# K and V transposed by one crossbar DMA per head and batch, in place of TensorE and VectorE, in the forward and backward of two attention blocks

## The chip, the cores and the metric

The kernel runs on one core of one Trainium2 chip. The metric is the device time of one execution in microseconds (us). The kernel before takes 1850.8 us (median of four runs, 1850.6 to 1851.6). Executions of one kernel mostly agree within 0.3%. Ratios in this text are computed as the mean time of one kernel's fast runs over the mean of the other's fast runs of the same rounds, so they are not quite the ratio of the medians quoted beside them.

Names: PE is TensorE (matrix products), DVE is VectorE, ACT is ScalarE, POOL is GpSimd, SP is SyncE. SP computes nothing here: it issues DMAs, in order. "SPq" in a profile is SP's instruction queue. The packets of every queue are recorded on the same 16 DMA engines, with the number of their queue (q1 is SP's, q0 GpSimd's). "Rings" in this text is the author's word for the packets of a queue that wait there; no record shows how full they are. L243 is line 243 of the kernel whose profile is shown; the numbers shift a little from kernel to kernel.

## The reference, cut to what matters

Two independent attention blocks A and B of the same shape, forward and backward. Per block there are B = 8 batches, H = 32 heads, 96 queries, 512 keys, Dh = 128, D = 640, all bfloat16.

```python
def _A_ref(x, k_cache, v_cache, wq, wo):
    q = (x @ wq).reshape(B, Sq, H, Dh).transpose(0, 2, 1, 3)
    scores = jnp.einsum("bhqd,bhkd->bhqk", q, k_cache) * (Dh ** -0.5)
    p = softmax(scores)
    o = jnp.einsum("bhqk,bhkd->bhqd", p, v_cache)
    return o.transpose(0, 2, 1, 3).reshape(B, Sq, H * Dh) @ wo
# outputs: concat(A, B), and the gradients of x, k_cache, v_cache, wq, wo of each block
```

There are 2 x 32 x 8 = 512 pairs of a head and a batch. Each needs its K and V both as loaded (keys on the partitions) and transposed (Dh on the partitions), because the products that give the scores and dP contract over Dh.

## The kernel before

The kernel is a software pipeline. Every (head, batch) passes through stages s1 to s8, one "tick" apart, and a scheduler then fixes the order of the instructions on each engine. The parts that the change and the argument touch:

```python
def c_ld(h, b):                       # SP's queue: two loads of 128 KB
    K_sb = kvp.tile([128, KC, 128], BF16, name="K_sb", bufs=11)
    V_sb = kvp.tile([128, KC, 128], BF16, name="V_sb", bufs=8)
    nc.sync.dma_start(K_sb[:], kc[b, h].rearrange("(p c) d -> p c d", c=KC))
    nc.sync.dma_start(V_sb[:], vc[b, h].rearrange("(p c) d -> p c d", c=KC))
def c_s1(h, b):                       # eight PE transposes, one DVE copy
    kvT_ps = bank([128, 2 * Sk], BF16, "kvT_ps")
    for c in range(KC):
        nc.tensor.transpose(kvT_ps[:, c * 128:(c + 1) * 128], st["K_sb"][:, c, :], ident[:])
    for c in range(KC):
        nc.tensor.transpose(kvT_ps[:, Sk + c * 128:Sk + (c + 1) * 128], st["V_sb"][:, c, :], ident[:])
    KVT = wk.tile([128, 2 * Sk], BF16, name="KVT", bufs=5)
    nc.vector.tensor_copy(KVT[:], kvT_ps[:])
    # ... st["KT"], st["VT"] are the halves of KVT
def c_s2a(h, b):                      # the first use of KVT
    nc.tensor.matmul(S_ps[:], hs["QT_h"][:, tok], st["KT"], start=True, stop=True)
    # ...
def c_s6(h, b):                       # the last use of KVT
    nc.tensor.matmul(dP_ps[:], hs["dOT_h"][:, tok], st["VT"], start=True, stop=True)
    # ...
def c_s4(h, b):                       # c_s7 does the same for dK
    # ... dV_ps by PE
    nc.scalar.activation(dV_sb[:], dV_ps[:], ACT.Identity, scale=1.0)
    nc.sync.dma_start(dv[b, h].rearrange("(p c) d -> p (c d)", c=KC), dV_sb[:])   # SP's queue again
```

So SP issues four DMAs of 128 KB for each head and batch: loads of K and V, stores of dV and dK. GpSimd's queue carries the weights, dwq, dwo and the outputs.

Of the kernel before, what the change touches and what calls it, by code (L numbers as in the profile page):

```python
# [11 lines left out]
BF16 = mybir.dt.bfloat16  # L12
# [32 lines left out]
OFF = dict(ld=0, s1=2, s2=3, s3=3, s4=4, s5=5, s6=6, s7=7, s8=8)  # L45
# [5 lines left out]
SLOTS = dict(LOAD=0, S2A=5, S2B=5.5, S1=6, S8=10, S7=20, S5=30, S4=40, S6=50, S3A=52, S3B=53, S5B=54, HEAD=SL_HEAD, GRP=SL_GRP)  # L51


def build_block(tc, em, tick0, blk, x, kc, vc, wq, wo, g_all, out_all, dx, dk, dv, dwq, dwo, ident, ones, pools, HG=8, first=True, groups=None):
    nc = tc.nc
    B, Sq, D = x.shape
    _, H, Sk, Dh = kc.shape
# [5 lines left out]
    KC = Sk // 128  # L63
# [28 lines left out]
    const, ps, kvp, wk, hd, hst, grp = (pools[k] for k in ("const", "ps", "kvp", "wk", "hd", "hst", "grp"))  # L92

    def bank(shape, dt, name):
        return ps.tile(shape, dt, name=name, tag="bank")
# [4 lines left out]
    CS = pools["CS"]  # L100
# [62 lines left out]
    def pA(h):  # L163
        def f():
            wo_h = hd.tile([128, D], BF16, name="wo_h", bufs=1)
            nc.gpsimd.dma_start(wo_h[:], wo[h * 128:(h + 1) * 128, :])
            wq_h = hd.tile([128, DC, 128], BF16, name="wq_h", bufs=1)
            with nc.allow_non_contiguous_dma(reason="per-head wq slice"):
                nc.gpsimd.dma_start(wq_h[:], wq_v[:, :, h * 128:(h + 1) * 128])
            HS[(blk, h)] = dict(wo_h=wo_h, wq_h=wq_h)  # L170
        return f

    def pB(h):
        def f():
            st = HS[(blk, h)]
            woT_ps = bank([128, DC * 128], BF16, "woT_ps")
            for c in range(DC):
                nc.tensor.transpose(woT_ps[:, c * 128:(c + 1) * 128], st["wo_h"][:, c * 128:(c + 1) * 128], ident[:])
            woT_h = hd.tile([128, DC * 128], BF16, name="woT_h", bufs=1)
            evac(EV["pB0"], woT_h[:], woT_ps[:])  # L180
            st["woT_h"] = woT_h
            wqT_ps = bank([128, DC * 128], BF16, "wqT_ps")
            for c in range(DC):
                nc.tensor.transpose(wqT_ps[:, c * 128:(c + 1) * 128], st["wq_h"][:, c, :], ident[:])
            wqT_h = hst.tile([128, D], BF16, name="wqT_h")
            evac(EV["pB1"], wqT_h[:], wqT_ps[:])
            st["wqT_h"] = wqT_h
            st["OT_h"] = hst.tile([128, T], BF16, name="OT_h")
            st["dQT_h"] = hst.tile([128, T], BF16, name="dQT_h")
            st["QT_h"] = hd.tile([128, T], BF16, name="QT_h")  # L190
            st["dOT_h"] = hd.tile([128, T], BF16, name="dOT_h")
        return f

    def pC(h, which, si):
        def f():
            st = HS[(blk, h)]
            (t0, w) = tsplits[si]
            if which == 0:
                dst = st["QT_h"]
                lhs = lambda c: st["wq_h"][:, c, :]  # L200
                rhsT = S["xT"]
                sc = scale
            else:
                dst = st["dOT_h"]
                lhs = lambda c: st["woT_h"][:, c * 128:(c + 1) * 128]
                rhsT = S["gT"]
                sc = None
            q_ps = bank([128, w], F32, "q_ps")
            for c in range(DC):
                nc.tensor.matmul(q_ps[:], lhs(c), rhsT[:, c, t0:t0 + w], start=(c == 0), stop=(c == DC - 1))  # L210
            evac(EV["pC%d%d" % (which, si)], dst[:, t0:t0 + w], q_ps[:], sc)
        return f
# [15 lines left out]

    def c_ld(h, b):
        def f():  # L230
            K_sb = kvp.tile([128, KC, 128], BF16, name="K_sb", bufs=11)
            V_sb = kvp.tile([128, KC, 128], BF16, name="V_sb", bufs=8)
            nc.sync.dma_start(K_sb[:], kc[b, h].rearrange("(p c) d -> p c d", c=KC))
            nc.sync.dma_start(V_sb[:], vc[b, h].rearrange("(p c) d -> p c d", c=KC))
            CS[(blk, h, b)] = dict(K_sb=K_sb, V_sb=V_sb)
        return f

    def c_s1(h, b):
        def f():
            st = CS[(blk, h, b)]  # L240
            kvT_ps = bank([128, 2 * Sk], BF16, "kvT_ps")
            for c in range(KC):
                nc.tensor.transpose(kvT_ps[:, c * 128:(c + 1) * 128], st["K_sb"][:, c, :], ident[:])  # L243
            for c in range(KC):
                nc.tensor.transpose(kvT_ps[:, Sk + c * 128:Sk + (c + 1) * 128], st["V_sb"][:, c, :], ident[:])  # L245
            KVT = wk.tile([128, 2 * Sk], BF16, name="KVT", bufs=5)
            nc.vector.tensor_copy(KVT[:], kvT_ps[:])  # L247
            st["KT"] = KVT[:, 0:Sk]
            st["VT"] = KVT[:, Sk:2 * Sk]
        return f  # L250

    def c_s2a(h, b):
# [23 lines left out]
    def c_s3a(h, b):  # L276
        def f():
            with tc.high_priority(PRIO_OFF):
                st = CS[(blk, h, b)]
                rinv = wk.tile([Sq, 1], F32, name="rinv", bufs=3)  # L280
                nc.vector.reciprocal(rinv[:], st["rowsum"][:])  # L281
                st["rinv"] = rinv
        return f
# [214 lines left out]
    for g in range(NG):  # L498
        h0 = GH0[g]
        for hh in range(groups[g]):  # L500
            h = h0 + hh
            c0t = tick0 + h * B
            em.add(c0t + HK["pA"], SL_LOAD, pA(h))
            em.add(c0t + HK["pB"], SL_HEAD, pB(h))
            for si in range(NTS):
                em.add(c0t + HK["pC0"][min(si, len(HK["pC0"]) - 1)], SL_HEAD, pC(h, 0, si))
                em.add(c0t + HK["pC1"][min(si, len(HK["pC1"]) - 1)], SL_HEAD, pC(h, 1, si))
            em.add(c0t + HK["pD1"], SL_HEAD, pD(h, 1))
            em.add(c0t + HK["pD0"], SL_HEAD, pD(h, 0))
            for b in range(B):  # L510
                ct = c0t + b
                em.add(ct + OFF["ld"], SLOTS["LOAD"], c_ld(h, b))
                em.add(ct + OFF["s1"], SLOTS["S1"], c_s1(h, b))
                em.add(ct + OFF["s2"], SLOTS["S2A"], c_s2a(h, b))
                em.add(ct + OFF["s2"], SLOTS["S2B"], c_s2b(h, b))
                em.add(ct + OFF["s3"], SLOTS["S3A"], c_s3a(h, b))
                em.add(ct + OFF["s3"], SLOTS["S3B"], c_s3b(h, b))
                em.add(ct + OFF["s5"], SLOTS["S5B"], c_s5b(h, b))
                em.add(ct + OFF["s4"], SLOTS["S4"], c_s4(h, b))
                S45.setdefault(ct + OFF["s5"], [None, None, None])[0] = (blk, h, b)  # L520
                S45.setdefault(ct + OFF["s4"], [None, None, None])[1] = (blk, h, b)
                S45.setdefault(ct + OFF["s6"], [None, None, None])[2] = (blk, h, b)
                S78.setdefault(ct + OFF["s8"], [None, None])[0] = (blk, h, b)
                S78.setdefault(ct + OFF["s7"], [None, None])[1] = (blk, h, b)
                em.add(ct + OFF["s6"], SLOTS["S6"], c_s6(h, b))
                em.add(ct + OFF["s7"], SLOTS["S7"], c_s7(h, b))
            em.add(c0t + HK["qA0"], SL_HEAD, qA(h, 0))
            for di in range(len(dsplits)):
                em.add(c0t + HK["qB"][min(di, len(HK["qB"]) - 1)], SL_HEAD + 1, qB(h, di))
            em.add(c0t + HK["qA1"], SL_HEAD, qA(h, 1))  # L530
            qd_parts = HK["qD"]
            for (k_, c_lo, c_hi) in qd_parts:
                if c_lo < DC:
                    em.add(c0t + k_, SL_HEAD + 2, qD(h, c_lo, min(c_hi, DC)))
        cLg = tick0 + (h0 + groups[g] - 1) * B + B - 1
        gs0 = max(3, (GSPREAD0 * groups[g]) // HG)
        gs1 = max(3, (GSPREAD1 * groups[g]) // HG)
        em.add(cLg + OFF["s5"] - 2, SL_LOAD, gW(g))
        subs = [(0, t, gi) for t in range(TT) for gi in range(len(gsplits))] + [(1, t, gi) for t in range(TT) for gi in range(len(gsplits))]
        n_out = TT * len(gsplits)  # L540
        for i, (which, t, gi) in enumerate(subs):
            if which == 0:
                tk = cLg + OFF["s5"] + 2 + (i * gs0) // n_out
            else:
                tk = cLg + OFF["s8"] + 2 + gs0 - 3 + ((i - n_out) * gs1) // n_out
            em.add(tk, SL_GRP, gU(g, which, t, gi))
# [119 lines left out]
```

## Time and profile before

| | before |
|---|---|
| time | 1850.8 us |
| PE busy | 1818 us, 98% of the span |
| DVE, ACT busy | 1519 us, 1434 us |
| packet time of the DMA engines (SP's and GpSimd's queues) | 46.2% + 10.7% of 16 engines |
| SP: DMAs issued, recorded issue time, gaps between issues | 2050, 843 us, 971 us |

The last row is summed from all records of SP in the trace. "Issue time" is what the profile records for a DMA instruction on SP's queue. It is not the time of the transfer: here a load of K is recorded for 0.34 us, and its data has landed 2.4 us after the issue began (medians). A "gap" is the time between two such records, so it holds SP's waits.

Lines of the page of the kernel before: busy time of each engine, the packets' time of the two large DMA queues, and the engines' shares of the chain of waits that ended last.

```profile
PE 1818.4 (98%) x26595; PEld 1571.4 (85%) x26744; DVE 1518.6 (82%) x3309; ACT 1434.4 (78%) x4041; POOL 777.9 (42%) x1378
...
q1 hardware_dynamic: 296480, 270.53, 46.2%
q0 software_dynamic: 19872, 60.32, 10.7%
...
PE 95%; POOL 2%; issue 1%; DVE 1%; DMA 1%; ACT 0%; POOLq 0%; SPq 0%; ACTq 0%
```

PE is busy 98% of the span, and the chain runs through PE for 95% of it. No other engine bounds the kernel.

Two pieces of the chain in order of time (start in us, duration in us, what): one group of transposes of K, one of V.

```profile
902.45 0.22 PE kvT_ps L243 x4
902.67 0.22 PE kvT_ps L245 x4
```

A group of four costs 0.22 us of the chain, so K and V together cost 0.445 us for each head and batch. The costliest-groups part of the page calls a transpose 219 ns, but the records of consecutive transposes overlap: they start 56 ns apart (median). The chain is the place to read what one costs.

SP's timeline of the kernel before (start in us, issue time in us, line, operation, destination and source):

```profile
104.59 0.38 SPq L234 DMA_DIRECT2D V_sb<-in_A_v_cache_dram  x1
105.06 0.38 SPq L397 DMA_DIRECT2D out_dram<-dK_sb  x1
106.08 0.34 SPq L333 DMA_DIRECT2D out_dram<-dV_sb  x1
106.59 0.34 SPq L233 DMA_DIRECT2D K_sb<-in_A_k_cache_dram  x1
107.16 0.34 SPq L234 DMA_DIRECT2D V_sb<-in_A_v_cache_dram  x1
107.75 0.34 SPq L397 DMA_DIRECT2D out_dram<-dK_sb  x1
```

An undisturbed issue is 0.34 us, one right behind another 0.38 us. Between most of them SP has time to spare.

### The profile page before, as it was taken

The page shows a single profiled execution, that of the slowest core. Times are in us where ns is not written, and L with a number is a line of the kernel's source. Part 1 is how long each engine was busy: PE and PEld are TensorE (multiplying, and loading weights), DVE is VectorE, ACT ScalarE, POOL GpSimd, SP SyncE. Part 2 cuts the span into 40 slices and gives each one's busy share as a digit, 9 for nine tenths or more (in the row PEclk, how much of TensorE's full clock was granted, in tenths as well). Part 3 has the DMA queues.
Part 4 walks back from the last instruction along what each step waited for, and adds up shares of the span by engine and source line. Part 5 has one row for each costly group of instructions (what it writes and reads, how often), then busy time and mean ns, then how long its engine had stood idle before and what let it go on. Part 6 is the DMA issues. An engine that isn't in the chain of part 4 may idle for free.

```text
span 1848.8 us, 69797 instructions
## 1 busy us (share of the span) xinstructions
PE 1818.4 (98%) x26595; PEld 1571.4 (85%) x26744; DVE 1518.6 (82%) x3309; ACT 1434.4 (78%) x4041; POOL 777.9 (42%) x1378
## 2 busy tenths in 40 slices
PE   6999999999999999999999999999999999999998
PEld 5888888888888888888888888888888888888887
DVE  5888867888788887888878887678887888878885
ACT  4888877888668886788767888788876788767882
POOL 4444433444334443345455444334433444333435
PEclk9999999999999999999999999999999999999999
DMA  7666654666546655566575665456655566555652
GB/s 229 196 193 202 192 162 149 199 195 193 164 148 194 201 183 165 159 191 205 186 229 173 196 194 184 160 167 198 192 175 164 171 196 199 159 165 176 201 168 84
DMA packets 316688, 335.32 MB, mean 181 GB/s; under 512 B 38368, under 2 KB 302048, under 8 KB 316352
## 3 DMA queue, kind: packets, MB, share of 16 engines
q1 hardware_dynamic: 296480, 270.53, 46.2%
q0 software_dynamic: 19872, 60.32, 10.7%
q8 instruction: 210, 3.44, 0.8%
q14 instruction: 126, 1.03, 0.2%
HBM read 171.57 MB, written 159.12 MB: 179 GB/s over the span
## 4 chain that ended last, share of the span: by engine, by line
PE 95%; POOL 2%; issue 1%; DVE 1%; DMA 1%; ACT 0%; POOLq 0%; SPq 0%; ACTq 0%
PE q_ps L210 11%; PE o_ps L480 10%; PE dV_ps L330 6%; PE kvT_ps L243 6%; PE kvT_ps L245 6%; PE dK_ps L394 6%; PE dP_ps L352 6%; PE S_ps L259 6%; PE dwq_ps L445 6%; PE dwo_ps L425 5%; PE optp_ps L313 5%; PE dq_dst_ps L377 5%; PE optp_ps L306 5%; PE dq_dst_ps L370 5%; PE n_ps L225 3%; PE nat_ps L410 2%
## 5 line engine op out<-in xcount | busy, mean ns | idle before, releaser
L290 POOL TENSOR_SCALAR P_sb<-E_sb,rinv 96x512 bf16<-96x512 bf16 x512 | 354.2, 692 | 780.5 <-DVE rinv L281 775.2
L271 ACT ACTIVATE E_sb<-S_ps,negm 96x512 bf16<-96x512 f32 x512 | 349.1, 682 | 291.2 <-DVE negm L261 288.1
L356 DVE SCALAR_TENSOR_TENSOR dS_sb<-dP_ps,dl_ps,P_sb 96x512 bf16<-96x512 f32 x512 | 383.3, 749 | 108.1 <-PE dl_ps L354 103.1
L247 DVE COPY KVT<-kvT_ps 128x1024 bf16<-128x1024 bf16 x512 | 350.0, 684 | 70.7 <-PE kvT_ps L245 69.0
L261 DVE TENSOR_REDUCE negm<-S_ps 96x1 f32<-96x512 f32 x512 | 347.6, 679 | 35.8 <-PE S_ps L259 30.1
L332 ACT ACTIVATE dV_sb<-dV_ps 128x512 bf16<-128x512 f32 x512 | 313.3, 612 | 0.0
L396 ACT ACTIVATE dK_sb<-dK_ps 128x512 bf16<-128x512 f32 x512 | 300.5, 587 | 15.7 <-PE dK_ps L394 12.9
L319 ACT ACTIVATE PT_sb<-optp_ps 128x384 bf16<-128x384 bf16 x512 | 253.4, 495 | 0.0
L245 PE MATMUL kvT_ps<-ident,V_sb 128*128 128x128 bf16 x2048 | 198.0, 219 | 0.0
L394 PE MATMUL dK_ps<-Qnat_h,dS_sb 96*128 96x128 bf16 x2048 | 197.9, 219 | 0.0
L243 PE MATMUL kvT_ps<-ident,K_sb 128*128 128x128 bf16 x2048 | 197.9, 219 | 0.0
L330 PE MATMUL dV_ps<-dOnat_h,P_sb 96*128 96x128 bf16 x2048 | 197.9, 219 | 0.0
L259 PE MATMUL S_ps<-KVT,QT_h 128*96 128x512 bf16 x512 | 193.8, 379 | 2.2 <-DVE KVT L247 1.9
L352 PE MATMUL dP_ps<-KVT,dOT_h 128*96 128x512 bf16 x512 | 195.2, 381 | 0.0
L342 POOL TENSOR_TENSOR prod<-OT_h,dOT_h 128x96 bf16<-128x96 bf16 x512 | 186.2, 364 | 19.4 <-ACT OT_h L316 14.4
L243 PEld LDWEIGHTS <-K_sb 128*128 128x128 bf16 x2048 | 147.3, 98 | 36.9 <-issue 1.9
L379 DVE COPY dST_sb<-dq_dst_ps 128x384 bf16<-128x384 bf16 x512 | 175.4, 343 | 1.8 <-PE dq_dst_ps L377 0.8
L313 PE MATMUL optp_ps<-ident,P_sb 96*128 96x96 bf16 x2048 | 171.6, 205 | 2.3 <-POOL P_sb L290 2.0
L377 PE MATMUL dq_dst_ps<-ident,dS_sb 96*128 96x96 bf16 x2048 | 172.1, 206 | 0.5 <-DVE dS_sb L356 0.4
L306 PE MATMUL optp_ps<-PT_sb,V_sb 128*128 128x96 bf16 x2048 | 172.1, 206 | 0.0
L370 PE MATMUL dq_dst_ps<-dST_sb,K_sb 128*128 128x96 bf16 x2048 | 170.7, 206 | 0.0
L445 PE MATMUL dwq_ps<-dQnat,x_nat 128*128 128x128 bf16 x1920 | 143.2, 219 | 0.0
(84 smaller groups left out, 3949.8 us busy)
## 6 DMA issues: line engine op xcount, KB each, us to landing
out_dram<-dV_sb SPq DMA_DIRECT2D x512, 128.0 KB, 2.0
out_dram<-dK_sb SPq DMA_DIRECT2D x512, 128.0 KB, 2.3
K_sb<-in_A_k_cache_dram SPq DMA_DIRECT2D x256, 128.0 KB, 2.4
V_sb<-in_A_v_cache_dram SPq DMA_DIRECT2D x256, 128.0 KB, 2.5
K_sb<-in_B_k_cache_dram SPq DMA_DIRECT2D x256, 128.0 KB, 2.4
V_sb<-in_B_v_cache_dram SPq DMA_DIRECT2D x256, 128.0 KB, 2.5
out_dram<-dwq_sb POOLq DMA_DIRECT2D x64, 160.0 KB, 3.0
out_dram<-dwo_sb POOLq DMA_DIRECT2D x64, 160.0 KB, 2.7
```

The source lines that it names most:

```text
L243: nc.tensor.transpose(kvT_ps[:, c * 128:(c + 1) * 128], st["K_sb"][:, c, :], ident[:])
L245: nc.tensor.transpose(kvT_ps[:, Sk + c * 128:Sk + (c + 1) * 128], st["V_sb"][:, c, :], ident[:])
L247: nc.vector.tensor_copy(KVT[:], kvT_ps[:])
L259: nc.tensor.matmul(S_ps[:], hs["QT_h"][:, tok], st["KT"], start=True, stop=True)
L261: nc.vector.tensor_reduce(negm[:], S_ps[:], axis=AX.X, op=ALU.max, negate=True)
L271: nc.scalar.activation(E_sb[:], st["S_ps"][:], ACT.Exp, bias=st["negm"][:], scale=1.0, accum_out=rowsum[:])
L290: nc.gpsimd.tensor_scalar(P_sb[:], st["E_sb"][:], st["rinv"][:], 0.0, op0=ALU.mult, op1=ALU.add)
L330: nc.tensor.matmul(dV_ps[:, c * 128:(c + 1) * 128], P_sb[:, c * 128:(c + 1) * 128], hs["dOnat_h"][:, b * 128:(b + 1) * 128], start=True, s ...
L332: nc.scalar.activation(dV_sb[:], dV_ps[:], ACT.Identity, scale=1.0)
L352: nc.tensor.matmul(dP_ps[:], hs["dOT_h"][:, tok], st["VT"], start=True, stop=True)
L356: nc.vector.scalar_tensor_tensor(dS_sb[:], dP_ps[:], dl_ps[:, 0:1], st["P_sb"][:], op0=ALU.subtract, op1=ALU.mult)
L394: nc.tensor.matmul(dK_ps[:, c * 128:(c + 1) * 128], dS_sb[:, c * 128:(c + 1) * 128], hs["Qnat_h"][:, b * 128:(b + 1) * 128], start=True, s ...
```

## The change

The intent is to take 512 x 0.445 = 228 us off the engine that bounds the kernel, and a copy of 684 ns off DVE each time, by letting the DMA crossbar transpose K and V together from SBUF to SBUF. The core of the diff:

```diff
-            K_sb = kvp.tile([128, KC, 128], BF16, name="K_sb", bufs=11)
-            V_sb = kvp.tile([128, KC, 128], BF16, name="V_sb", bufs=8)
-            nc.sync.dma_start(K_sb[:], ...)
-            nc.sync.dma_start(V_sb[:], ...)
+            KV_sb = kvp.tile([128, 2, KC, 128], BF16, name="KV_sb", bufs=11)
+            nc.sync.dma_start(KV_sb[:, 0], ...)
+            nc.sync.dma_start(KV_sb[:, 1], ...)
 ...
-            kvT_ps = bank([128, 2 * Sk], BF16, "kvT_ps")
-            ... eight nc.tensor.transpose
-            KVT = wk.tile([128, 2 * Sk], BF16, name="KVT", bufs=5)
-            nc.vector.tensor_copy(KVT[:], kvT_ps[:])
+            KVT = kvp.tile([128, 2 * KC, 128], BF16, name="KVT", bufs=6)
+            nc.sync.dma_start_transpose(KVT[:], st["KV_sb"][:].rearrange("p a c d -> p (a c d)"))
 ...
-                em.add(ct + OFF["s1"], SLOTS["S1"], c_s1(h, b))
+                em.add(ct + OFF["s1"] - 1, SLOTS["LOAD"], c_s1(h, b))
```

More of the change, by code (lines that the diff above doesn't have):

```diff
@@ L230, in f @@
         def f():
-            K_sb = kvp.tile([128, KC, 128], BF16, name="K_sb", bufs=11)
-            V_sb = kvp.tile([128, KC, 128], BF16, name="V_sb", bufs=8)
-            nc.sync.dma_start(K_sb[:], kc[b, h].rearrange("(p c) d -> p c d", c=KC))
-            nc.sync.dma_start(V_sb[:], vc[b, h].rearrange("(p c) d -> p c d", c=KC))
-            CS[(blk, h, b)] = dict(K_sb=K_sb, V_sb=V_sb)
+            KV_sb = kvp.tile([128, 2, KC, 128], BF16, name="KV_sb", bufs=11)
+            nc.sync.dma_start(KV_sb[:, 0], kc[b, h].rearrange("(p c) d -> p c d", c=KC))
+            nc.sync.dma_start(KV_sb[:, 1], vc[b, h].rearrange("(p c) d -> p c d", c=KC))
+            CS[(blk, h, b)] = dict(K_sb=KV_sb[:, 0], V_sb=KV_sb[:, 1], KV_sb=KV_sb)
         return f
@@ L240, in f @@
             st = CS[(blk, h, b)]
-            kvT_ps = bank([128, 2 * Sk], BF16, "kvT_ps")
-            for c in range(KC):
-                nc.tensor.transpose(kvT_ps[:, c * 128:(c + 1) * 128], st["K_sb"][:, c, :], ident[:])
-            for c in range(KC):
-                nc.tensor.transpose(kvT_ps[:, Sk + c * 128:Sk + (c + 1) * 128], st["V_sb"][:, c, :], ident[:])
-            KVT = wk.tile([128, 2 * Sk], BF16, name="KVT", bufs=5)
-            nc.vector.tensor_copy(KVT[:], kvT_ps[:])
-            st["KT"] = KVT[:, 0:Sk]
-            st["VT"] = KVT[:, Sk:2 * Sk]
+            KVT = kvp.tile([128, 2 * KC, 128], BF16, name="KVT", bufs=6)
+            nc.sync.dma_start_transpose(KVT[:], st["KV_sb"][:].rearrange("p a c d -> p (a c d)"))
+            st["KT"] = KVT[:, 0:KC].rearrange("p c k -> p (c k)")
+            st["VT"] = KVT[:, KC:2 * KC].rearrange("p c k -> p (c k)")
         return f
```

## The prediction

> **What bounds it now.** TensorE. The page's first part has PE busy 98% of 1848.8 us, and the chain of waits that ended last is 95% PE, with no other engine above 2%. PE waits under 20 us in total (waits of PE), nearly all at the start. VectorE is busy 1519 us, ScalarE 1434 us. The 16 DMA engines are busy 58% (SP's queue 46.2%, GpSimd's 10.7%). A head and batch (512 of them) takes 3.6 us, of which 3.2 between the group updates (timeline).
>
> **What is removed.** Eight TensorE transposes: the chain shows each four at 0.22 us, so 0.445 us x 512 = 228 us, all on the critical path. The copy of KVT, 684 ns x 512 = 350 us of VectorE, hardly on it. One of the eight PSUM banks is used one step less. If nothing else bound, PE would need about 1621 us; ScalarE's 1434 us is then 88%, VectorE's is 1169 us.
>
> **What is added.** 512 crossbar transposes of 128x1024 bf16 (256 KB), all on SP's in-order queue, which already issues four DMAs per head and batch. Two terms:
>
> 1. DMA engines. The 1 KB packets took 50.7 ns, so a 128 KB copy costs 128 x 50.7 / 16 = 0.41 us of all 16 engines; with GpSimd's transfers a head and batch costs 2.07 us. No trace shows a transpose. The Trainium skill (DMA: Bandwidth & Descriptors, Latency and other measured facts) gives 261 GB/s for one kernel: an estimate of 1.0 us each. Sum 3.1 us: 1570 us in all, 97% of a 1621 us span.[...]
>
> 2. SP's issuing. The SP timeline shows copies issued back to back every 0.46 us (0.34 us recorded; every fifteenth or so takes 1 to 1.7 us). Four are 1.85 us, with the long ones 2.0. For a transpose from SBUF, the same page (its table of cycles before and after, column for previous generations) gives 262,144 cycles for 8,192 tiles, 32 a tile; 128x1024 has 64 tiles of 16x128, hence an estimate of 1.7 us at 1.2 GHz, perhaps more. Sum 3.7 us per head and batch: 1900 us.
>
> Also the transpose waits on SP itself for its loads to land (2.4 us after issue now) and for a KVT buffer; outputs queue behind it. The order of the built program shows each DMA also waiting on the DMA eight before it, so a slow transpose holds the line.
>
> **Net.** PE stops being the limit; SP's queue and the DMA engines take over. I expect 3.8 us per head and batch, about 1930 us; 8 in 10 between 1690 and 2350. Faster by over 2%: 0.27; within 2%: 0.13; slower by over 2%: 0.60.
>
> **What the profile would show.** Right: L243/L245 and the KVT copy gone; PE near 1590 us busy but at 80 to 85% of the span, with idle time before S_ps released by the DMA KVT<-KV_sb; SP's timeline nearly solid, transposes recorded at 1.5 us or more; DMA share above 85%; issue to landing of K and V well above 2.4 us; the chain through SP's queue and DMA. Wrong: transposes recorded under 1.2 us with SP idle, chain still over 90% PE, span near 1630 to 1680 us.
>
> **What would make it wrong.** Transposes cheap to issue, or moved at near copy speed while other traffic flows: then 1650 us, bound by PE and ScalarE. On the other side, a transpose that stops other traffic on the rings while it drains would push past 2200 us. Slack from six KVT buffers may hide latency, but not a saturated queue.

## The result, and the profile after

The changed kernel takes 2066.3 us (median of four runs, 2065.2 to 2083.1) against 1850.8 us. The ratio is 1.118, with a 95% interval of 1.1145 to 1.1222. It is slower by 12%. The outputs are correct.

| | before | after |
|---|---|---|
| PE busy | 1818 us (98%) | 1729 us (84%) |
| packet time, SP's and GpSimd's queues | 46.2% + 10.7% | 88.1% + 10.7% |
| SP: DMAs issued | 2050 | 2562 |
| SP: recorded issue time | 843 us | 1756 us |
| SP: gaps between issues | 971 us | 272 us |

The same lines of the page of the changed kernel, and the chain by line:

```profile
PE 1729.1 (84%) x22648; PEld 1406.6 (68%) x22648; DVE 1258.4 (61%) x2797; ACT 1416.0 (69%) x4041; POOL 776.4 (38%) x1378
...
q1 hardware_dynamic: 837152, 404.82, 88.1%
q0 software_dynamic: 19872, 60.32, 10.7%
...
PE 52%; DMA 40%; issue 2%; ACT 2%; DVE 1%; POOL 1%; SPq 0%; POOLq 0%; ACTq 0%; DVEq 0%
DMA KVT<-KV_sb 39%; PE q_ps L210 9%; PE o_ps L474 8%; PE S_ps L253 6%; PE dK_ps L388 4%; PE dwq_ps L439 3%; PE dV_ps L324 3%; PE dP_ps L346 3%; PE dq_dst_ps L371 3%; PE dq_dst_ps L364 3%; PE optp_ps L300 3%; PE optp_ps L307 3%; PE dwo_ps L419 2%; PE n_ps L225 1%; PE nat_ps L404 1%
```

Who waited for whom (waiting engine and line, what it waited for: us in total, times, longest):

```profile
PEld L253 <- DMA KVT<-KV_sb: 351.8, 205, 10.3
...
DVE negm L255 <- PE S_ps L253: 305.5, 212, 10.6
PE S_ps L253 <- DMA KVT<-KV_sb: 296.8, 173, 10.1
```

PE now waits for the transposes: 297 us before the matmul S_ps, with the weight load before it. DVE waits in turn for S_ps. Before, nothing of this size stood in front of PE. A part of the chain in order of time, after:

```profile
907.65 0.17 PE S_ps L253
907.83 3.60 DMA KVT<-KV_sb
911.43 0.04 issue
911.47 0.42 PE S_ps L253
```

PE ends one S_ps at 907.82 us, SP starts a transpose at 907.83, its data has landed 3.6 us later, and the next S_ps starts at once. The profile's chain puts the whole 3.6 us down to the DMA, the issue on SP included. What held SP until 907.83 us is in SP's own timeline, after:

```profile
903.86 1.24 SPq L241 DMA_TRANSPOSE KVT<-KV_sb  x1
905.19 0.58 SPq L391 DMA_DIRECT2D out_dram<-dK_sb  x1
905.87 0.40 SPq L327 DMA_DIRECT2D out_dram<-dV_sb  x1
906.36 0.41 SPq L232 DMA_DIRECT2D KV_sb<-in_A_k_cache_dram  x1
906.82 0.44 SPq L233 DMA_DIRECT2D KV_sb<-in_A_v_cache_dram  x1
907.35 0.39 SPq L391 DMA_DIRECT2D out_dram<-dK_sb  x1
907.83 1.24 SPq L241 DMA_TRANSPOSE KVT<-KV_sb  x1
```

SP stands in issues almost without a pause. A transpose takes 1.24 us to issue, the copy behind it 0.58 us, the others some 0.4 us, and 0.05 to 0.10 us lies between two. Over the whole run the records add to 1756 us of issue and 272 us of gaps, 2028 of 2063 us. The loads of a transpose had landed 9.3 us before it was issued (median), so what it waited for was its turn. (The profile's list of SP's waits names more, 941 us in all. But 821 us of that lie inside issue records, in which a transpose takes a median of 1.24 us here and 1.23 us in the bare stream below, where SP waits for no engine.) The page's DMA row shows nines in nearly all of its slices too. So the profile offers two suspects, SP's queue (theory S) and the 16 engines (theory E), and a third, that the transposes are issued too late and that only their latency counts (theory L).

### The profile page after: what moved, and what is told of

It reads as the page before. It is cut to its first block, busy times and chain, and to the rows that moved or that the text cites. A ratio compares the mean times of both kernels' runs of the same rounds, so it can differ in the third digit from the quotient of the medians.

```text
span 2063.4 us, 61963 instructions
## 1 busy us (share of the span) xinstructions
PE 1729.1 (84%) x22648; PEld 1406.6 (68%) x22648; DVE 1258.4 (61%) x2797; ACT 1416.0 (69%) x4041; POOL 776.4 (38%) x1378
## 3 DMA queue, kind: packets, MB, share of 16 engines
q1 hardware_dynamic: 837152, 404.82, 88.1%
q0 software_dynamic: 19872, 60.32, 10.7%
## 4 chain that ended last, share of the span: by engine, by line
PE 52%; DMA 40%; issue 2%; ACT 2%; DVE 1%; POOL 1%; SPq 0%; POOLq 0%; ACTq 0%; DVEq 0%
DMA KVT<-KV_sb 39%; PE q_ps L210 9%; PE o_ps L474 8%; PE S_ps L253 6%; PE dK_ps L388 4%; PE dwq_ps L439 3%; PE dV_ps L324 3%; PE dP_ps L346 3%; PE dq_dst_ps L371 3%; PE dq_dst_ps L364 3%; PE optp_ps L300 3%; PE optp_ps L307 3%; PE dwo_ps L419 2%; PE n_ps L225 1%; PE nat_ps L404 1%
## 5 line engine op out<-in xcount | busy, mean ns | idle before, releaser
L253 PE MATMUL S_ps<-KVT,QT_h 128*96 128x512 bf16 x512 | 210.4, 411 | 308.2 <-DMA KVT<-KV_sb 296.8
L253 PEld LDWEIGHTS <-QT_h 128*96 128x96 bf16 x512 | 63.4, 124 | 354.6 <-DMA KVT<-KV_sb 351.8
L388 PE MATMUL dK_ps<-Qnat_h,dS_sb 96*128 96x128 bf16 x2048 | 208.2, 227 | 0.0
L324 PE MATMUL dV_ps<-dOnat_h,P_sb 96*128 96x128 bf16 x2048 | 206.3, 225 | 0.0
L371 PE MATMUL dq_dst_ps<-ident,dS_sb 96*128 96x96 bf16 x2048 | 180.4, 212 | 1.6 <-DVE dS_sb L350 1.5
L300 PE MATMUL optp_ps<-PT_sb,KV_sb 128*128 128x96 bf16 x2048 | 180.0, 212 | 0.1
L364 PE MATMUL dq_dst_ps<-dST_sb,KV_sb 128*128 128x96 bf16 x2048 | 179.0, 212 | 0.0
L364 PEld LDWEIGHTS <-KV_sb 128*128 128x128 bf16 x2048 | 141.4, 102 | 42.7 <-issue 12.2
L156 ACT ACTIVATE QT_h<-q_ps 128x512 bf16<-128x512 f32 (+1 forms) x128 | 64.9, 507 | 137.5 <-PE q_ps L210 137.3
L210 PE MATMUL q_ps<-xT,wq_h 128*128 128x512 bf16 (+1 forms) x640 | 150.1, 358 | 0.1
```

Source lines behind the costliest of these rows:

```text
L210: nc.tensor.matmul(q_ps[:], lhs(c), rhsT[:, c, t0:t0 + w], start=(c == 0), stop=(c == DC - 1))
L324: nc.tensor.matmul(dV_ps[:, c * 128:(c + 1) * 128], P_sb[:, c * 128:(c + 1) * 128], hs["dOnat_h"][:, b * 128:(b + 1) * 128], start=True, s ...
L364: nc.tensor.matmul(dQT_ps, st["K_sb"][:, c, :], st["dST_sb"][:, c * Sq:(c + 1) * Sq], start=(c == 0), stop=(c == KC - 1))
L388: nc.tensor.matmul(dK_ps[:, c * 128:(c + 1) * 128], dS_sb[:, c * 128:(c + 1) * 128], hs["Qnat_h"][:, b * 128:(b + 1) * 128], start=True, s ...
```

## The experiments

Kernels marked "one look" ran once, beside a run of the kernel before on the same chip; a single run on one core is of unknown state. All others ran two to four times and were compared by fast runs alone.

### The stream alone: t_alone, stream, stream_not, stream_actq (one look each, wrong outputs on purpose)

All compute is removed and only DMAs are left. t_alone issues 512 transposes of one tile. stream issues, for each head and batch, the loads, the stores and the transpose (of the batch loaded three before). stream_not leaves the transposes out. stream_actq issues them from ACT's queue.

```diff
+ for each head and batch:
+     nc.sync.dma_start(KV_sb[:, 0], kc...); nc.sync.dma_start(KV_sb[:, 1], vc...)
+     nc.sync.dma_start(dk..., src[:, 0])
+     nc.sync.dma_start_transpose(KVT[:], <KV_sb of three batches ago>)   # stream_not: left out
+     nc.sync.dma_start(dv..., src[:, 1])                                 # stream_actq: nc.scalar for the transpose
```

> 512 transposes of the same 128x1024 tile back to back on SP's queue, nothing else (wrong outputs on purpose). Theory A, the transpose itself costs the DMA engines the 1.8 us that its packets summed to in the changed kernel: about 920 us, 256-byte packets again near 28 ns. Theory B, by itself it costs about 1.15 us of the engines (18 ns a packet, the median of the changed kernel) and the rest is collisions with other traffic: bound by SP's issue of 1.24 us plus the gap of 0.09 us, about 680 us, packets near 18 ns.

> Only SP's stream of the changed kernel: two loads, two stores and one transpose for each head and batch, no compute, no transfers of GpSimd (wrong outputs on purpose). If the DMA engines or SP's queue are the limit in the changed kernel, compute hardly matters: 1900 to 2000 us. If SP's bare issue is the limit (4 x 0.46 + 1.33 us): 1620 us. If the changed kernel is held by latency (the transposes issued late behind stores that wait for ScalarE), this stream runs well below 1800 us, and the packets of 256 bytes near 18 to 20 ns.

> The same stream without the transposes: 2048 copies. By the engines' packet time 2048 x 0.41 = 840 us, by SP's issue 2048 x 0.46 = 940 us; so about 950 us. It gives what the transposes add to the stream, by difference: 1.8 us each if theory A, 1.15 to 1.3 us each if theory B.

> The stream with the transposes issued from ScalarE's queue, so that SP issues copies alone. If SP's issuing limits the stream, it falls to the engines' time (1.64 + 1.15 us, 1430 us); if the DMA engines do, it stays as the stream on one queue, or gets longer because the transposes now meet copies on another ring.

| kernel | time | per head and batch | SP: issue + gaps |
|---|---|---|---|
| t_alone | 714 us | 1.39 us | 682 + 26 us |
| stream_not | 1028 us | 2.0 us | 925 + 97 us |
| stream | 1741 us | 3.4 us | 1615 + 120 us |
| stream_actq | 1541 us | 3.0 us | 1004 + 531 us (SP), 663 us (ACT) |

Seven consecutive transposes of t_alone, merged by the timeline (start, duration, what), and one cycle of the stream on SP's queue:

```profile
499.52 9.59 SPq L573 DMA_TRANSPOSE KVT<-src  x7
```

```profile
503.48 1.24 SPq L584 DMA_TRANSPOSE KVT<-KV_sb  x1
504.76 0.59 SPq L585 DMA_DIRECT2D out_dram<-src  x1
505.40 0.44 SPq L577 DMA_DIRECT2D KV_sb<-in_A_k_cache_dram  x1
505.88 0.44 SPq L578 DMA_DIRECT2D KV_sb<-in_A_v_cache_dram  x1
506.36 0.43 SPq L580 DMA_DIRECT2D out_dram<-src  x1
506.84 1.27 SPq L584 DMA_TRANSPOSE KVT<-KV_sb  x1
```

Alone a transpose costs 1.38 us (708 us from first to last issue over 512), not the 1.8 us that its packets add up to in the changed kernel (1024 packets of 28.1 ns over 16 engines). In t_alone the same packets took 21.3 ns. So the packets' time is no measure of what a transpose costs by itself, which refutes theory A of the expectation; the 714 us are nearer to theory B's 680, with issues recorded at 1.33 us and not 1.24. The 509 transposes add 713 us to the copies' 1028, 1.40 us each: on one queue the two simply add. (The copies alone took 1028 us where 950 were expected.) And SP is solid in the stream (1735 of 1739 us). With the transposes issued from another queue, the same bytes take 200 us less, though not the 310 us less that were expected. So the engines can do the same work in 3.0 us for each head and batch or less, and the 3.4 us on one queue belong to that queue. Whether to its issuing or to its packets, which all stand behind one another, this pair does not show: stream_actq moves both. The experiments that follow separate them.

The stream's 1741 us lies between what the expectations allowed: compute, or something that comes with it, costs the changed kernel another 324 us.

### Same bytes, other issues: pair_loads and stores_gpsimd; other bytes, same issues: half_stores

pair_loads joins the loads of two batches in one DMA (and has two fewer of a setup tile, for the room):

```diff
-            nc.sync.dma_start(KV_sb[:, 0], kc[b, h].rearrange("(p c) d -> p c d", c=KC))
+            if b % 2 == 0:   # one tile for two batches
+                nc.sync.dma_start(KV2[:, :, 0], kc[b:b + 2, h].rearrange("b (p c) d -> p b c d", c=KC))
```

stores_gpsimd moves both stores to GpSimd's queue (`nc.sync` to `nc.gpsimd` in c_s4 and c_s7). half_stores stores only columns 0 to 255 of dV and dK, which is wrong on purpose:

```diff
-            nc.sync.dma_start(dv[b, h].rearrange("(p c) d -> p (c d)", c=KC), dV_sb[:])
+            nc.sync.dma_start(dv[b, h].rearrange("(p c) d -> p (c d)", c=KC)[:, 0:256], dV_sb[:, 0:256])
```

> The changed kernel with the loads of two batches joined into one DMA of 256 KB (same bytes, 512 issues of SP fewer). Theory S, SP's in-order issuing is the limit (1756 us of recorded issue plus 272 us of gaps in a 2063 us span): each issue saved is worth 0.5 to 0.6 us, 512 of them 260 to 310 us; about 1780 us. Theory E, the 16 DMA engines are the limit: bytes and packets are the same, so 2040 to 2070 us. Theory L, the latency of a transpose issued too late: in between, as the transposes move forward in the queue.

> The changed kernel, but dK and dV stored for half of their columns only (wrong outputs on purpose): the same number of DMAs on SP, 67 MB less for the engines (about 0.4 us of all engines for each head and batch). Theory E: 200 us less, about 1860 us. Theory S: the number of issues is unchanged, only issues that were stretched by full rings get shorter: 1980 to 2050 us.

> The changed kernel with the stores of dK and dV issued from GpSimd's queue in place of SP's: same bytes, SP left with two loads and one transpose (about 2.7 us for each head and batch). Theory S: the limit moves to the DMA engines or PE, 1750 to 1850 us. Theory E: no gain, 2050 us or more. Rival of both, collisions of GpSimd's packets with the transposes: longer than 2100 us.

| kernel | time | against before | SP: issue + gaps |
|---|---|---|---|
| changed kernel | 2066 us | 1.118 | 1756 + 272 us |
| half_stores | 2036 us | 1.100 | 1727 + 268 us |
| pair_loads | 1974 us | 1.068 | 1648 + 286 us |
| stores_gpsimd | 1854 us | 1.0015 (0.9995 to 1.0035) | 1412 + 387 us |

Taking away 67 MB of the stores gives 30 us, where theory E expected 200; the number of packets stayed the same. Moving the stores' issues to another queue, with not a byte less, gives 212 us (1854 us, at the edge of what theory S expected), where theory E expected nothing. But GpSimd's queue moved the stores in 32768 packets of 4 KB in place of 131072 of 1 KB, so stores_gpsimd changes the packets as well as the issuer. pair_loads has no such flaw: queue and data packets are those of the changed kernel (8192 packets of 4 bytes fewer, an estimate of 5 us by their 9.5 ns), and 512 issues fewer give 93 us. Theory E is refuted as the first limit of the changed kernel, though the page's DMA row showed nines throughout.

pair_loads missed theory S's number: 93 us instead of about 290. SP did lose 512 issues, but its other issues grew: the mean transpose from 1.39 to 1.56 us, the mean store of dV from 0.54 to 0.64 us, and SP stayed solid. What SP saved came back in part as longer issues. The reading that fits is that an issue gets longer when the rings are full, so that the engines stand close behind SP as the second limit. This is argued and not shown. How much it could be in the changed kernel can be estimated: with every transpose at its shortest record (1.237 us) and every copy at 0.34 us, the 1756 us of issue would be 1330, so some 426 us are of issues longer than the shortest. half_stores took 29 us of them away. stores_gpsimd agrees with the reading. There SP has 298 us of gaps longer than 0.2 us, yet a transpose takes a median of 5.7 us from issue to landing (4.0 in the changed kernel) and PE still waits for it:

```profile
PE S_ps L253 <- DMA KVT<-KV_sb: 123.0, 125, 3.1
```

So even with SP relieved, the full change does no better than the kernel before: 1854 us. That the rings are what holds it there is argued from these latencies, not shown by an experiment of its own.

### What an issue of a transpose costs: k_only and split_T

k_only transposes K by the crossbar and V by PE and DVE, so that a transpose has half the size. split_T leaves the changed kernel alone but issues each transpose as two halves:

```diff
-            nc.sync.dma_start_transpose(KVT[:], st["KV_sb"][:].rearrange("p a c d -> p (a c d)"))
+            nc.sync.dma_start_transpose(KVT[:, 0:KC], st["K_sb"].rearrange("p c d -> p (c d)"))
+            nc.sync.dma_start_transpose(KVT[:, KC:2 * KC], st["V_sb"].rearrange("p c d -> p (c d)"))   # k_only: by PE and DVE
```

> K transposed by the crossbar for every batch, V by TensorE: as many crossbar bytes and as little TensorE work as every2, but 512 crossbar instructions of half the size in place of 256. Theory S with a fixed cost of some 1.2 us to issue a transpose, whatever its size: 256 x 1.3 us more of SP than every2, so SP is solid again at 1890 to 1960 us. If the cost lies in the bytes (theory E): 1800 us, as every2.

> The changed kernel with each transpose of 128x1024 issued as two of 128x512: the same bytes and packets, the same work on TensorE, 512 issues of SP more. Fixed cost of an issue (1.19 us recorded for the half size in k_only, 1.24 for the whole): 512 x 1.3 us more, 2650 to 2750 us. Cost by bytes: 2060 to 2100 us. In between: part of each.

k_only took 2340 us (1.265), outside both expectations. Its question stayed open there: the scheduler had placed each transpose three DMAs behind the load of its K in SP's queue (16 behind the load of its V in the changed kernel; medians in the traces), and SP stood still for the load to land. The waits of SP's own queue in k_only:

```profile
SPq L241 <- DMA KV_sb<-in_A_k_cache_dram: 231.7, 241, 9.1
SPq L241 <- DMA KV_sb<-in_B_k_cache_dram: 225.0, 255, 4.9
```

That is 457 us of a queue that stores and loads stand in too; ACT then waited 534 us for its stores. So the failure is put down to the order and not to the transpose; no run changed the order alone.

split_T took 2681 us (1.449), inside what a fixed cost of an issue expects (2650 to 2750). With the same bytes and the same PE work, 512 more issues cost 614 us, 1.2 us each. SP's recorded issue grew by as much, from 1756 to 2369 us (gaps 278 us, so SP is solid in 2647 of 2683 us), while the packet time of SP's queue fell from 88.1% to 62.1% of the engines. There the issues are the limit and the engines are not. SP's timeline of split_T shows the half-size issues:

```profile
906.38 1.20 SPq L241 DMA_TRANSPOSE KVT<-KV_sb  x1
907.63 1.25 SPq L242 DMA_TRANSPOSE KVT<-KV_sb  x1
908.98 0.53 SPq L328 DMA_DIRECT2D out_dram<-dV_sb  x1
909.60 0.38 SPq L232 DMA_DIRECT2D KV_sb<-in_A_k_cache_dram  x1
```

An issue of half the size is recorded with a median of 1.20 us against 1.24 us for the whole (1.19 in k_only). Between these two sizes the cost to SP hardly depends on the bytes.

### What lies between the stream and the kernel: stream_pool and lite_pool

stream_pool (one look, wrong outputs on purpose) adds 256 transfers of 160 KB on GpSimd's queue to the stream. lite_pool is the changed kernel with the head's weights loaded once for each block and dwo and dwq stored for the last head alone, also wrong on purpose: 41 MB less on GpSimd's queue.

```diff
 def pA(h):                                        # lite_pool
+    if h > 0:
+        HS[(blk, h)] = dict(wo_h=HS[(blk, 0)]["wo_h"], wq_h=HS[(blk, 0)]["wq_h"]); return
 ...
-            if st["dwo_n"] == len(dsplits):
+            if st["dwo_n"] == len(dsplits) and h == H - 1:   # and the same for dwq
```

> The bare stream (1739 us on SP's queue) plus GpSimd's share of transfers: four of 160 KB for each head, 256 in all, 42 MB (wrong outputs on purpose). If SP's issuing alone bounds the stream, transfers of another queue cost it nothing: 1740 us. If they stall the transposes that they meet (in the changed kernel a transpose that met one took 2.37 us from first to last packet, against 1.59 us of those that met neither these nor instruction fetches), 0.8 us or more each: 1850 to 1950 us, transposes' and stores' issues stretched.

> The changed kernel without most of GpSimd's transfers: the weights of a head loaded once for each block, dwo and dwq stored for the last head alone (wrong outputs on purpose); some 41 MB of 60 MB gone, SP's and TensorE's work unchanged. From stream_pool, 129 us for 42 MB: about 1935 us. If SP's queue is indifferent to other queues' traffic: 2060 us.

stream_pool took 1870 us, 129 us more than the stream. The transposes that met one of GpSimd's packets spread over 3.8 us from first to last packet, the others over 1.8 us, so another queue's traffic goes with slower transposes, and SP's issue time is 107 us longer than in the stream. But in stream_pool GpSimd ran ahead and packed its transfers together, and in the kernel they matter less: lite_pool took 2035 us, 31 us less than the changed kernel and not 129. I had carried the number over from a denser stream, and that failed.

The account of the 324 us between the two profiled spans, from SP's records of the stream and of the changed kernel:

| | stream | changed kernel | difference |
|---|---|---|---|
| issue time | 1615 us | 1756 us | 141 us |
| gaps between issues | 120 us | 272 us | 152 us |
| before the first and after the last issue | 4 us | 35 us | 31 us |
| span | 1739 us | 2063 us | 324 us |

The gaps: the median is 44 ns in the stream and 93 ns in the changed kernel. In the stream, SP's trace holds 7 separate semaphore instructions; in the changed kernel 2031: most DMAs there wait for two things, an earlier DMA and an engine. In the changed kernel itself, a gap with such an instruction in it has a median of 93 ns (2018 gaps) and one without it 52 ns (543 gaps). The longer issues: the transposes account for 71 us (1.39 against 1.25 us), the copies for the rest. lite_pool puts some 30 us of the whole down to GpSimd's transfers. In lite_pool, transposes that met only a packet of instruction fetches (134) spread over 2.36 us, those that met nothing (350) over 1.58 us. That makes fetches a candidate for the rest, but no run took them away, and this stays open. (An instruction fetch is a DMA that brings program code; q8 in the profile.)

### A part of the change: every2, every2_deep, every2_gp2, five8_gp2 and before_gp2

every2 uses the crossbar for even batches alone and PE and DVE for the others:

```diff
+ def by_dma(h, b): return b % 2 == 0
  def c_s1(h, b):
+     if by_dma(h, b): nc.sync.dma_start_transpose(KVT[:], st["KV_sb"][:].rearrange("p a c d -> p (a c d)"))
+     else:            # eight nc.tensor.transpose into kvT_ps, then nc.vector.tensor_copy to KVT, as before
```

every2_deep gives it a seventh KVT buffer and a fourth of dV_sb and dK_sb (and two fewer of a setup tile, for the room). every2_gp2 is every2 with the stores on GpSimd's queue. five8_gp2 takes five of eight batches (0, 2, 3, 5, 6). before_gp2 is the kernel before with the stores on GpSimd's queue.

> Crossbar transposes for every second batch alone, TensorE and VectorE as before for the others. SP then needs 4 x 0.6 + 0.75 us, 3.15 us, the engines about 2.7 us, PE 1849 - 114 us: theories S and E both expect it to be bound by PE, 1735 to 1760 us, faster than both kernels. If a transpose's latency is what holds the chain (theory L), each second batch still waits, and the time stays above 1850 us.

> every2 with a seventh KVT buffer and a fourth buffer each for dV_sb and dK_sb. In every2 PE still idles 66 us, 44 of it before S_ps, and ScalarE waits 37 us for stores. If that is slack, 30 to 50 us come back: 1760 us. If the rings or SP are simply late, nothing changes: 1800 us.

> every2 with all dK and dV stores on GpSimd's queue: SP is left with two loads and half a transpose for each head and batch (1.8 us of 3.4). Theory S: the waits for KVT vanish, 1750 us, bound by PE. If GpSimd's packets stall the transposes more than SP's relief is worth: above 1804 us.

> The kernel before with only the stores of dK and dV moved to GpSimd's queue, as in every2_gp2. TensorE is busy 98% of the kernel before and idles 19 us, so this can give nothing: 1845 to 1870 us. If it runs near 1767 us, the gain of every2_gp2 was the stores' and not the transposes'.

> every2_gp2 with five of eight batches on the crossbar in place of four. TensorE needs 28 us less; if it is still the limit, 1740 us. The kernel with all eight and the same queues (stores_gpsimd) took 1854 us and waited 123 us for KVT, so the best share lies somewhere between; if the engines' rings are already full at five of eight, 1770 us or more.

| kernel | time | against before | PE waits for KVT from the crossbar |
|---|---|---|---|
| every2 | 1804 us | 0.975 (0.9735 to 0.9768) | 36 us |
| every2_deep | 1816 us | 0.981 (0.9797 to 0.9826) | not better: PE idles 77 us in all, every2 66 us |
| every2_gp2 | 1767 us | 0.955 (0.9533 to 0.9565) | none of note |
| five8_gp2 | 1775 us | 0.962 (0.9557 to 0.9678) | PE idles 56 us in all, every2_gp2 34 us |
| before_gp2 | 1858 us | 1.004 (1.0019 to 1.0059) | no crossbar |

every2 is faster than both kernels, but not by what was expected (1735 to 1760): SP still waits and is waited for. Theory L expected it to stay above 1850 us, and it does not, so the latency of a late transpose is not the first limit. every2_deep shows that more buffers do not help by themselves. In its trace each transpose stands six DMAs behind its own load, where every2 has eleven, and it starts 0.3 us after the load landed, where every2 has 4.2 us (medians). The scheduler had spent the room on another order; that this order is what cost the 12 us is likely and not shown. every2_gp2 frees SP (875 us of issue in all), the waits of PE for the crossbar vanish, and PE is the limit again. The busy line of the page of every2_gp2:

```profile
PE 1717.4 (97%) x24547; PEld 1461.5 (83%) x24696; DVE 1387.5 (79%) x3053; ACT 1417.2 (80%) x4041; POOL 1339.6 (76%) x2402
```

It is 4.5% faster than the kernel before, 17 us short of the 1750 us expected. before_gp2 shows that moving the stores gains nothing while PE bounds: the gain is the transposes' and the moved stores only let it through. At five of eight, PE's work should have fallen by another 28 us; its busy time fell by 10 us (1717 to 1707), its idle time grew by 21, and the time is no better. A higher share was not worth it on these queues.

## Why the prediction was wrong, point by point

**What bounds the kernel before: right.** PE, at 98% busy and 95% of the chain. before_gp2 confirms that relief of SP's queue gives nothing there.

**What is removed: right.** In every2_gp2, where half of the transposes are gone and PE is still the limit, PE's busy time fell by 101 us, near the 114 us that half of the sum stands for. DVE's busy time fell by 260 us in the changed kernel; the copies' 350 us had overlapped other records in part. There PE's fell by only 89 us, to 1729 and not to the predicted 1590. The trace shows much of the reason: for 206 us of the changed kernel the granted TensorE clock, the share of its full speed that the profile records, is half (its mean is 0.951, against 0.999 in the kernel before), 176 us of PE's busy time lie in these stretches, and a matmul of dK_ps took 309 ns in them and 219 ns outside. If work there took 1.4 to 2 times as long, that is 50 to 88 us of the missing 139, by estimate; the rest stays open. The prediction had no term for the clock. It is not what bounds the changed kernel, in which PE waits for the transposes. The relief was real, but the limit had moved.

**Where the limit goes: right.** The prediction named SP's queue and the DMA engines, and put SP's sum above that of the engines. SP is solid in the changed kernel, and pair_loads, half_stores and split_T show that issues and not bytes bound it. One sign that it had named failed: it expected transposes recorded at 1.5 us or more, and their median is 1.24 us. The Trainium skill's Perfetto Trace Analysis (What "DMA-bound" means) lists this as a case of its own: the issuing engine's sequencer track is solid with DMA slices, which is the making of descriptors and not the moving of data. This trace agrees: issues fill 1756 us of 2063, and of the 272 us between them only 63 us lie in gaps longer than 0.2 us.

**How large: wrong. The step that failed is the sum of "2. SP's issuing".** The prediction had 2.0 us for four copies and 1.7 us for a transpose, 3.7 us in all, and rounded it up to 3.8. Measured, with the mean gap of 0.106 us counted to each issue:

| SP, for each head and batch | predicted | measured |
|---|---|---|
| four copies | 2.0 us | 4 x (0.510 + 0.106) = 2.46 us |
| one transpose | 1.7 us | 1.387 + 0.106 = 1.49 us |
| sum | 3.7 us | 3.96 us, 512 of them 2028 us |

The copies were sized too small, by 0.46 us, or 236 us in all. The 0.46 us between starts was read from copies behind copies. A copy behind a transpose is recorded at 0.64 us on average in the changed kernel, and at 0.60 us in the bare stream, against 0.47 and 0.44 us of the others: such a place does not occur in the kernel before, so its trace could not show it. That is 0.17 us of the 0.46. The other 0.29 us, the larger part, are spread over all copies: even one that follows a copy takes 0.47 + 0.11 us with its gap, where the prediction had 0.50 with the long ones. What lengthens these stays open; fuller rings are a guess. The transpose was sized too large, by 0.21 us, or 108 us: the number of tiles, from which it was worked out, has almost no part in it (split_T). The two errors have opposite signs, and that the second took away half of the first was luck. Together they left the prediction some 130 us short, and +4% was forecast where +12% came. The range held the result.

**The engines' term.** 3.1 us were predicted with GpSimd's traffic. stream_actq shows at most 3.0 us without that traffic, which fits; no run measured the term itself. The expected sign "DMA share above 85%" came true and proves nothing: half_stores cut 67 MB and gave 30 us. stores_gpsimd's two queues add to 74.6% + 33.8%, more than all engines have, so the records of packets overlap and the share is no measure of how much room is left.

**Waits on SP itself and the eight DMAs in flight.** They were named as further costs. In the changed kernel SP hardly waits at all (gaps over 0.2 us: 63 us in total), so they were not the cause here. In k_only the first of them was: 457 us.

## What to carry to other kernels

In this case a DMA that replaced work of the bounding engine had two prices, engine time for its bytes and issue time on the queue that launches it, and the second added up in order with everything else that the queue launched. So count the issues per iteration, with their gaps, before counting bytes. Where a queue becomes the limit, move other DMAs off it, or move only as much work as it has room for; here half of the transposes with the stores on another queue gave 4.5%, while all of them on one queue lost 12%. Where a DMA waits for another one on the same queue, look at how far apart the scheduler has placed the two.

## What the Trainium skill lacked or had wrong

- DMA: Bandwidth & Descriptors (Issuing engines are not separate DMA queues) says that issuing from several engines saves only the sequencer's time, "which is usually small relative to the DMA itself". Here that time was the limit: moving 1024 stores to another queue, same bytes (in larger packets), took 212 us off 2066, and 512 issues fewer on the same queue, same bytes, 93 us.
- DMA: Bandwidth & Descriptors, the table of cycles before and after: 32 cycles a tile for a transpose from SBUF, in the column for previous generations, gave the prediction's estimate of 1.7 us for 64 tiles. The issue was recorded at 1.24 us for 64 tiles and 1.20 us for 32. No page gives a fixed issue time of a crossbar transpose from SBUF; the table's time for one instruction is for a transpose from HBM.
- The same page (Latency and other measured facts) gives 261 GB/s for a transpose, and Advanced Engine Details and Errata (X-Bar Transpose (TRN2)) 350 to 400 GB/s. Transposes of 256 KB from SBUF, back to back and alone, moved 262144 bytes every 1.38 us, a mean of 189 GB/s, with SP's queue solid. As SP was solid, this is what one queue reached and need not be the crossbar's own limit.
- No page says what a second semaphore to wait for costs a DMA's queue. In the changed kernel the median gap between issues was 93 ns with a separate semaphore instruction in it and 52 ns without; in the stream, with hardly any such instruction, 44 ns.
- No page says that an issue right behind a transpose is longer: 0.60 us on average for a copy there, 0.44 us for the others, in the bare stream.
- Perfetto Trace Analysis (Identifying the Most-Contended Engine) calls occupancy misleading for DMA, since there are 16 engines, but does not say that the summed packet time of the queues can pass 100% of them: 74.6% + 33.8% in stores_gpsimd.
